# First MLP block in two halves of f around the second block, weight conversion without GpSimd, float32 on the first sequence's way back

## The chip, the cores and the metric

The kernel runs on one core of a Trainium2 chip. The metric is the device time of one execution in microseconds (us); lower is better. Five engines work side by side, each through its own list of instructions in the order in which the program writes them: TensorE (PE, matrix products), VectorE (DVE), ScalarE (ACT), GpSimd (POOL) and SyncE (SP, which here only starts DMA transfers). DMA transfers are also started by ACT and POOL. A transfer that waits for a buffer holds up whatever stands behind it on the engine that starts it.

## The reference, cut to what matters

```python
X = np.fft.rfft(x, axis=1)                       # x: 4 sequences of 3008 x 256, float32
Yr = Xr @ w_r - Xi @ w_i + b_r                   # 256 x 256 weights, complex product
Yi = Xr @ w_i + Xi @ w_r + b_i
Y = soft_shrink(Yr, 0.01) + 1j * soft_shrink(Yi, 0.01)
y = np.fft.irfft(Y, n=3008, axis=1)              # back to 12032 tokens of 256
h = y @ w_in                                     # 256 -> 2048
out = (h * sigmoid(h)) @ w_out                   # 2048 -> 256
```

w_in and w_out arrive as float64 and are brought to float32 pairs on the chip.

## The kernel before, in words

Each sequence goes through the spectral part and then, as rows of tokens, through the MLP. The transform of length 3008 is done as 47 x 64 in two matrix stages on each side:

- **s1** (lines 166 to 189; s1_half for sequences 2 and 3): eight groups g per sequence, two halves of 512 columns each; result to the scratch scr1 in device memory.
- **s2** and **mix** (lines 236 to 273): twelve steps u per sequence; s2 reads 256 KB of scr1 (tile a) and a 128 KB table (t2), splits its result into a high and a low float32r part (xh, xl), and mix multiplies by the complex weights in 24 products of 256 columns. VectorE then adds the bias and shrinks (lines 270 to 272, y).
- **i1**, the first stage of the way back (lines 353 to 374): split_z cuts y into zh (ScalarE) and zl (GpSimd for the first sequence, line 358), six float32r products with a split table t3 (256 KB, started by POOL), result to the scratch scr2.
- **i2** (lines 414 to 446): reads scr2 by groups of four j (tile gin, 384 KB) and writes the tokens of one MLP block, 512 columns, as xt (high and low).

The **MLP** runs in 24 blocks of 512 tokens (the last is smaller) with 16 slices f of 128 hidden units each. One pair (block, f) is a *tick*. In tick t the program emits, in this order: split_g of tick t-1 (gh on ScalarE, gl on VectorE, lines 477 to 485), mlp1 of tick t (six products of 512 columns, sigmoid on ScalarE, g on VectorE, lines 459 to 475), the *fill* of the tick, and mlp2 of tick t-2 (four pairs of products into four accumulators `acc`, lines 489 to 523). After f = 15 the four accumulators are copied and added (lines 519, 520) and stored.

Only the first sequence's spectral part (b = 0) and s1 of the second stand ahead of the ticks, in a *prologue*: s1 of sequence 0, then a loop of twelve u_steps, then a tail with the last i1 steps, s1(1,2) to s1(1,7) and the i2 of block 0. All other spectral work is fill: `put` gives each piece the next tick that has none (the list `taken`), `at` names a tick outright.

**Weight conversion** (lines 536 to 571): w_in and w_out come in 16 units of 512 KB, loaded by SP into buffers of tag gin (four) or s1o (two). w_begin loads the next unit and begins the oldest loaded one (ScalarE, line 558); the first w_go does two VectorE operations (lines 560, 561), the second w_go two more (lines 566, 567), a copy to the high part on ScalarE (line 569) and two GpSimd operations for the low part (lines 570, 571). Units 0 to 7 (f = 0 to 7) are converted in the prologue, units 8 to 15 in ticks 0 to 12, by the list W_PLAN of (w_go, w_begin) counts. A block needs all 16 f, so tick 8 of block 0 already needs unit 8.

x of sequences 0 and 1 is loaded by POOL (x_ahead, line 154) into seven buffers, chosen by X_BUFS; two of these are x_sb[0], x_sb[1].

Of the kernel before, what the change touches and what calls it, by code (L numbers as in the profile page):

```python
# [26 lines left out]
BLK = 512  # L27
NFF = DFF // 128
W_PLAN = [(1, 1), (1, 1), (1, 0), (2, 1), (1, 1), (1, 0), (1, 1), (3, 1), (0, 0), (1, 0), (1, 1), (2, 0), (1, 0)]
# [3 lines left out]
X_BUFS = [0, 1, 2, 3, 4, 5, 6, 0, 1, 2, 3, 4, 5, 2, 1, 0]  # L33
# [3 lines left out]
def dft_tables():  # L37
# [16 lines left out]
    for h in range(2):  # L54
# [33 lines left out]
    c3l = c3 - c3h  # L88
    return {
# [3 lines left out]
        "c4": c4.reshape(96, NP).astype(np.float32),  # L93
    }
# [3 lines left out]
def spectral_mlp_kernel(ctx: ExitStack, tc: tile.TileContext, x, w_r, w_i, b_r, b_i, w_in, w_out, c1, c2, c3, c4, out):  # L98
# [67 lines left out]
    def s1(b, g, late=False):  # L166
        t = x_t.pop((b, g))
        if b == 1 and g > 4:
            o = x_pre[(4, 6, 2)[g - 5]][:96, :]
        else:  # L170
            tag, bufs = ("s1o", 2) if 8 * b + g in (6, 7, 10, 11, 12) else ("gin", 4)
            o = sb.tile([128, 4 * D], F32, tag=tag, bufs=bufs, name="s1o")[:96, :]
# [180 lines left out]
    def split_z(b, u):  # L353
# [4 lines left out]
        (nc.gpsimd if b == 0 and u < NU - 2 else nc.vector).tensor_sub(zl, y, zh)  # L358
        u_t[b, u] = (zh, zl)

    def i1(b, u):
        zh, zl = u_t.pop((b, u))
# [3 lines left out]
        for r in range(2):  # L366
            for n, (m, z) in enumerate(((0, zh), (0, zl), (1, zh))):
                nc.tensor.matmul(  # L368
                    out=pv[:, r, :], lhsT=t3[:, m, r * 128:(r + 1) * 128], rhs=z[:, r, :],
                    start=(n == 0), stop=(n == 2),  # L370
                )
# [42 lines left out]
    def i2(i, e):  # L414

        c0, n = BLOCKS[i]
        if e == 0:
            xt[i] = tuple(sb.tile([128, 2, BLK], F32R, tag=f"xt{k}", bufs=2, name=f"xt{k}") for k in range(2))
# [70 lines left out]
    def mlp2(i, f):  # L489
        n = BLOCKS[i][1]  # L490
        gh, gl = gf.pop((i, f))
        for t in range(n // 128):
            if f == 0:
                acc[i, t] = ps.tile([128, 512], F32, tag="acc", bufs=4, name="acc")
            a = acc[i, t]
            q = slice(t * 128, (t + 1) * 128)
            if i == LAST:
# [8 lines left out]
                start=(f == 0), stop=False,  # L506
# [3 lines left out]
                start=False, stop=(f == NFF - 1),  # L510
            )
        if f == NFF - 1:
# [23 lines left out]
    def w64_load(src):  # L536
        tag, bufs = ("s1o", 2) if len(weights) < 6 and len(weights) % 3 else ("gin", 4)
        t = sb.tile([128, 512, 2], U32, tag=tag, bufs=bufs, name="w64")
# [8 lines left out]
    def w64_split(t, shape, hi, lo):  # L547
# [3 lines left out]
        def shaped(a):  # L551
# [10 lines left out]
                                       op0=ALU.bitwise_and, op1=ALU.bitwise_or)  # L562
        yield
# [5 lines left out]
        nc.scalar.copy(hi, w)  # L569
        nc.gpsimd.tensor_sub(w, w, hi)  # L570
        nc.gpsimd.tensor_tensor(out=lo, in0=w, in1=shaped(lw), op=ALU.add)

    with tc.manual_schedule():
# [6 lines left out]
        x_pre.extend(sb.tile([128, 4 * D], F32, tag=f"xt{k}", bufs=2, name="x_pre") for k in (0, 0, 1, 1))  # L580
# [65 lines left out]
        def u_step(b, u):  # L646
            if u < NU:
                if u + (3 if b == 0 else 2) < NU:
                    u_load(b, u + (3 if b == 0 else 2))
                s2(b, u)  # L650
            if u > 0:
                t3_load(b, u - 1)
            if b == 0:
                if u > 2:
                    w_go()
                if u % 2:
                    w_begin()
# [22 lines left out]
        for u in range(NU):  # L680
            u_step(0, u)
# [3 lines left out]
            if 1 < u < 8:  # L685
# [27 lines left out]
        i2(0, 1)
        w_begin()
        state["prologue"] = False

        ticks = [(i, f) for i in range(len(BLOCKS)) for f in range(NFF)]
# [5 lines left out]
        taken = set(range(17, len(ticks), NFF))  # L723
# [9 lines left out]
        for i in range(1, len(BLOCKS)):  # L733
            at(16 * i - 9, i2_load, i)
            put(16 * i - 7, i2, i, 0)
            put(16 * i - 5, i2, i, 1)
# [69 lines left out]
```

## Time and profile before

| what | value |
|---|---|
| median of 3 runs | 1387.65 us (1385.81 to 1388.34) |
| the profiled execution's own time | 1388.13 us |
| its span in the trace | 1386.3 us |
| mean granted TensorE clock | 0.994 |
| PE busy | 1364.3 us, 98% |
| DVE / ACT / POOL busy | 65% / 51% / 12% |
| chain of waits, by engine | PE 89%, DVE 4%, DMA 3%, issue 2%, ACT 1% |

The span runs from the first to the last instruction; the 1.83 us between it and the execution's own time lie around it. A PE that is busy is not PE at its peak: products overlap, so their shown durations are longer than the distance from one start to the next, and the distance is what counts. A granted clock of 1.00 is 2.4 GHz, and 0.5 is 1.2 GHz.

### The profile page before, as it was taken

The numbers are of one execution on the slowest core, as the hardware profiler recorded it, in microseconds if no ns is written. First come the engines' busy times: TensorE is split into PE (matmuls) and PEld (weight loads), VectorE is DVE, ScalarE is ACT, GpSimd is POOL, SyncE is SP. The second block draws the span as 40 slices with busy tenths as digits, with TensorE's granted clock in tenths as the row PEclk, the third lists the DMA queues.
The fourth block names the chain that finished last, engine by engine and source line by source line (L and its number), as shares of the span: only waits on it lengthen the run. The fifth ranks groups of instructions, "written<-read, shape, count | busy, mean of one in ns | idle before, by whom it ended". The sixth has DMA issues, their size and how long they took to land.

```text
span 1386.3 us, 20474 instructions
## 1 busy us (share of the span) xinstructions
PE 1364.3 (98%) x7638; PEld 1169.3 (84%) x7638; DVE 898.2 (65%) x1485; ACT 711.2 (51%) x1394; POOL 170.0 (12%) x205
## 2 busy tenths in 40 slices
PE   7998999999999999999999999999999999999998
PEld 3976788888888888888888888888888888888888
DVE  3899868777655677767655577776654555455555
ACT  5565555555554555555454445455444444444444
POOL 2555411120100011111100011111000000000000
PEclk9999999999999999999999999999999999999999
DMA  8975232331423214233121121220210110011001
GB/s 250 318 230 172 76 100 83 96 92 42 124 76 85 58 35 114 69 114 80 46 77 41 33 76 51 84 81 24 61 27 16 27 39 9 19 27 39 1 16 24
DMA packets 69855, 105.09 MB, mean 76 GB/s; under 512 B 7228, under 2 KB 51388, under 8 KB 69756
## 3 DMA queue, kind: packets, MB, share of 16 engines
q1 hardware_dynamic: 55685, 75.18, 18.5%
q0 software_dynamic: 10496, 24.91, 7.1%
q10 hardware_dynamic: 3575, 3.70, 0.8%
q8 instruction: 60, 0.98, 0.3%
q14 instruction: 39, 0.32, 0.1%
HBM read 66.28 MB, written 37.49 MB: 75 GB/s over the span
## 4 chain that ended last, share of the span: by engine, by line
PE 89%; DVE 4%; DMA 3%; issue 2%; ACT 1%; POOL 0%; ACTq 0%; SPq 0%; DVEq 0%; POOLq 0%
PE h L466 36%; PE acc L504 24%; PE acc L508 12%; PE mix L324 6%; PE i L410 3%; PE s L299 2%; PE i L368 2%; PE s L164 2%; PE acc L499 1%; DVE ww L560 1%; PE mix L263 1%; DMA scr<-i1o 1%; PE i2e L410 1%; DMA x_pre<-in_x_dram 1%; DVE gl L484 1%
## 5 line engine op out<-in xcount | busy, mean ns | idle before, releaser
L466 PE MATMUL h<-xt,win 128*128 128x512 f32 (+1 forms) x2304 | 588.5, 391 | 1.8 <-ACT xt L443 1.6
L504 PE MATMUL acc<-wout,gh 128*128 128x512 f32 x1472 | 540.0, 401 | 0.0
L466 PEld LDWEIGHTS h<-xt,win 128*128 128x128 f32 x2304 | 403.4, 189 | 85.3 <-ACT xt L443 1.7
L473 ACT ACTIVATE g<-h 128x512 f32<-128x512 f32 (+1 forms) x385 | 226.5, 588 | 387.6 <-PE h L466 386.3
L474 DVE TENSOR_TENSOR g<-h,g 128x512 f32<-128x512 f32 (+1 forms) x385 | 261.4, 679 | 242.2 <-ACT g L473 238.9
L508 PE MATMUL acc<-wout,gl 128*128 128x256 f32 x1472 | 413.0, 281 | 4.8 <-DVE gl L484 4.8
L484 DVE TENSOR_TENSOR gl<-g,gh 128x512 fp32r<-128x512 f32 (+1 forms) x385 | 282.1, 733 | 174.8 <-ACT gh L483 170.4
L504 PEld LDWEIGHTS acc<-wout,gh 128*128 128x128 f32 x1472 | 277.4, 188 | 59.0
L483 ACT CAST gh<-g 128x512 fp32r<-128x512 f32 (+1 forms) x385 | 235.1, 611 | 156.0 <-DVE g L474 153.6
L508 PEld LDWEIGHTS acc<-wout,gl 128*128 128x128 f32 x1472 | 278.6, 189 | 16.1 <-DVE gl L484 7.2
L331 POOL TENSOR_TENSOR q<-q,bias 128x256 f32<-128x256 f32 x36 | 26.4, 733 | 672.7 <-ACT q L330 672.7
L344 DVE TENSOR_TENSOR y<-q,mix 64x256 f32<-64x256 f32 x144 | 60.3, 419 | 2.2
L410 PEld LDWEIGHTS i<-c_sb,gin 96*128 96x128 f32 x420 | 54.4, 191 | 6.6 <-issue 1.7
L410 PE MATMUL i<-c_sb,gin 96*128 96x94 f32 x420 | 53.9, 272 | 1.6 <-DMA gin<-scr 1.6
L368 PE MATMUL i<-zh,t 128*128 128x256 f32 x192 | 45.4, 298 | 0.0
L299 PEld LDWEIGHTS s<-t,a 128*128 128x128 f32 x288 | 37.7, 191 | 3.0
L299 PE MATMUL s<-t,a 128*128 128x128 f32 x288 | 37.9, 274 | 0.0
L164 PE MATMUL s<-sx,c 94*96 94x512 f32 (+1 forms) x120 | 35.5, 404 | 1.0 <-DVE sx L195 0.3
L368 PEld LDWEIGHTS i<-zh,t 128*128 128x128 f32 x192 | 33.1, 190 | 1.1 <-issue 0.5
L520 DVE TENSOR_TENSOR o<-acc,o 128x256 f32<-128x256 f32 x92 | 32.4, 415 | 0.0
L332 POOL TENSOR_TENSOR q<-q,bias 128x256 f32<-128x256 f32 x36 | 32.0, 888 | 2.8
L426 DVE TENSOR_TENSOR xt<-i,xt 128x376 fp32r<-128x376 f32 (+2 forms) x48 | 28.0, 584 | 6.1 <-ACT xt L425 6.0
(113 smaller groups left out, 1232.3 us busy)
## 6 DMA issues: line engine op xcount, KB each, us to landing
a<-scr SPq DMA_DIRECT2D x48, 256.0 KB
t<-in_c_dram POOLq DMA_DIRECT2D x48, 256.0 KB, 3.2
gin<-scr SPq DMA_DIRECT2D x32, 384.0 KB
scr<-s1o SPq DMA_DIRECT2D x28, 384.0 KB
x_sb<-in_x_dram POOLq DMA_DIRECT2D x25, 376.0 KB, 4.4
scr<-i1o SPq DMA_DIRECT2D x36, 256.0 KB
t<-in_c_dram SPq DMA_DIRECT2D x48, 128.0 KB
w<-in_moe_w_in_dram SPq DMA_DIRECT2D x8, 512.0 KB
```

The source lines that it names most:

```text
L164: nc.tensor.matmul(out=p[:96, :], lhsT=c1_hl[m][:K, :], rhs=hl[k][:K, :], start=(n == 0), stop=(n == 2))
L299: nc.tensor.matmul(out=pv[:, e, :, r, :], lhsT=a[:, r, e * 128:(e + 1) * 128], rhs=t2[:, r * 128:(r + 1) * 128], start=True, stop=True,)
L324: nc.tensor.matmul(out=out, lhsT=x_[:, e, c, :], rhs=m[:, e, :], start=(n == 0), stop=(n == 5))
L368: nc.tensor.matmul(out=pv[:, r, :], lhsT=t3[:, m, r * 128:(r + 1) * 128], rhs=z[:, r, :], start=(n == 0), stop=(n == 2),)
L410: nc.tensor.matmul(out=p[:, o:o + m], lhsT=g_t[b, j // 4][:, q:q + 128], rhs=c4_sb[:, p0:p0 + m], start=True, stop=True,)
L466: nc.tensor.matmul(out=p[:, :n], lhsT=w[:, e, f * 128:(f + 1) * 128], rhs=v[:, e, :n], start=(m == 0), stop=(m == 5),)
L473: nc.scalar.activation(out=g[:, q], in_=p[:, q], func=ACTF.Sigmoid)
L474: nc.vector.tensor_tensor(out=g[:, q], in0=p[:, q], in1=g[:, q], op=ALU.mult)
L483: nc.scalar.copy(gh[:, q], g[:, q])
L484: nc.vector.tensor_sub(gl[:, q], g[:, q], gh[:, q])
L504: nc.tensor.matmul(out=a, lhsT=gh[:, q], rhs=wout[:, f].rearrange("p a c -> p (a c)"), start=(f == 0), stop=False,)
L508: nc.tensor.matmul(out=a[:, D:2 * D], lhsT=gl[:, q], rhs=wout[:, f, 0, :], start=False, stop=(f == NFF - 1),)
```

## The change: what it does

- The order of ticks becomes block 0 with f = 0 to 7, block 1 with all 16 f, block 0 with f = 8 to 15, then blocks 2 and up as before. The sums of the first half (f = 0 to 7) are added and kept in x_sb[1] and added to those of the second half at tick 33. i2 of block 1 moves from ticks 9, 11, 13 to ticks 1, 3, 5.
- The conversion's two last operations go from GpSimd to VectorE, and its high copy moves one w_go earlier. The units 8 to 15 are spread over ticks 0 to 19 (W_GO, W_BEGIN; the later entries find nothing left). Every unit is loaded into a gin buffer.
- For sequence 0, i1 is one float32 product per half instead of three float32r products, with an unsplit table (128 KB, started by SP); split_z is left out for it. i1(u-2) now stands in step u, where i1(u-3) stood.
- s1(1,5), s1(1,6), s1(1,7) move from the prologue's tail into six ticks (0, 2, 4, 6, 7, 8) as s1_later.
- The x loads of (1,2) to (1,6) stand in steps 3 to 7 of the loop; with no other work on POOL between them. s1 of sequence 2 starts at tick 37 instead of 30, with a spacing of 6 instead of 7.

```diff
+W_GO = (0, 1, 3, 4, 6, 7, 8, 9, 10, 12, 13, 14, 15, 17, 18, 19, 20, 21, 22)
+W_BEGIN = (1, 4, 7, 9, 12, 14, 17, 19)
-X_BUFS = [0, 1, 2, 3, 4, 5, 6, 0, 1, 2, 3, 4, 5, 2, 1, 0]
+X_BUFS = [0, 1, 2, 3, 4, 5, 6, 0, 1, 2, 3, 4, 0, 2, 1, 0]
...
+    def s1_later(g, i):
+        t = x_t[1, g]
+        if i == 0:
+            x_t[1, g, "o"] = sb.tile([128, 4 * D], F32, tag="s1o", bufs=2, name="s1o")[:96, :]
+        o = x_t[1, g, "o"]
+        p = bank("s1")
+        q = slice(i * 512, (i + 1) * 512)
+        nc.tensor.matmul(out=p[:96, :], lhsT=c1_sb, rhs=t[:, q], start=True, stop=True)
+        nc.scalar.copy(o[:, q], p[:96, :])
+        if i:
+            v = scr1[1].rearrange("r (a j) d -> (r a) (j d)", a=4)
+            store(v[:, g * 4 * D:(g + 1) * 4 * D], o)
+            del x_t[1, g], x_t[1, g, "o"]
...
     def t3_load(b, u):
+        if b == 0:
+            t3_t[b, u] = sb.tile([128, 256], F32, tag="t3", bufs=5, name="t3f")
+            nc.sync.dma_start(out=t3_t[b, u], in_=c3f[:, u * 256:(u + 1) * 256])
+            return
...
     def i1(b, u):
...
         for r in range(2):
+            q = slice(r * 128, (r + 1) * 128)
+            if b == 0:
+                nc.tensor.matmul(out=pv[:, r, :], lhsT=t3[:, q], rhs=z[:, r, :], start=True, stop=True)
+                continue
...
     def mlp2(i, f):
+        begins = f == 0 or (i, f) == (0, 8)
+        ends = f == NFF - 1 or (i, f) == (0, 7)
...
+        if ends:
             for t in range(n // 128):
                 a = acc.pop((i, t))
+                half = x_sb[1][:, t * D:(t + 1) * D]
+                if f == 7:
+                    nc.scalar.copy(half, a[:, D:2 * D])
+                    nc.vector.tensor_tensor(out=half, in0=a[:, 0:D], in1=half, op=ALU.add)
+                    continue
...
+                if i == 0:
+                    nc.vector.tensor_add(o, o, half)
...
     def w64_split(t, shape, hi, lo):
...
+        nc.scalar.copy(hi, shaped(w.bitcast(F32)))
         yield
...
-        nc.scalar.copy(hi, w)
-        nc.gpsimd.tensor_sub(w, w, hi)
-        nc.gpsimd.tensor_tensor(out=lo, in0=w, in1=shaped(lw), op=ALU.add)
+        nc.vector.tensor_sub(w, w, hi)
+        nc.vector.tensor_tensor(out=lo, in0=w, in1=shaped(lw), op=ALU.add)
...
+        def u_step(u):
             if u < NU:
+                if u + 3 < NU:
+                    u_load(0, u + 3)
+                t3_load(0, u)
+                s2(0, u)
+            if u > 1:
+                w_go()
+            if 0 <= u - 1 < NU:
+                mix(0, u - 1)
+            if u % 2 and u < NU:
+                w_begin()
             if 0 <= u - 2 < NU:
+                i1(0, u - 2)
...
+        w_begin()
+        u_step(NU)
         s1(1, 2)
+        flush(1)
+        u_step(NU + 1)
+        i2_load(0)
+        w_tags[:] = [(("zl", 2), ("zh", 2))]
+        s1(1, 3)
         w_go()
+        flush(1)
+        s1(1, 4)
         w_go()
         w_begin()
         i2(0, 0)
         i2_ends(0)
+        w_go()
         i2(0, 1)
+        i2_load(1)
+        w_go()
         w_begin()
+        flush(1)
...
+        ticks = [(0, f) for f in range(8)] + [(1, f) for f in range(NFF)] + [(0, f) for f in range(8, NFF)]
+        ticks += [(i, f) for i in range(2, len(BLOCKS)) for f in range(NFF)]
...
+        taken = {9, 25} | set(range(33, len(ticks), NFF))
...
+        for t in W_GO:
+            at(t, w_go)
+        for t in W_BEGIN:
+            at(t, w_begin)
+        for g in (5, 6, 7):
+            for i in range(2):
+                t = put(0, s1_later, g, i)
+            if g == 5:
+                at(t, x_ahead)
+        for t in (11, 35):
             at(t, x_ahead)
...
-        for b, t0, dt in ((2, 30, 7), (3, 110, 8)):
+        for b, t0, dt in ((2, 37, 6), (3, 110, 8)):
```

## Rows read from the trace of the kernel before

**Rows 1.** Busy time by stretch: PE, PEld, DVE, ACT, POOL (count), clock, DMA share, GB/s

```profile
40.40:88.80 48.40, 47.45 (x394) 46.51 (x393) 45.68 (x61) 28.59 (x60) 33.29 (x34) 1.00 1.03 295
...
107.67:165.00 57.33, 52.00 (x233) 41.29 (x234) 52.09 (x70) 28.86 (x54) 32.70 (x23) 0.91 0.43 133
165.00:1386.30 1221.30, 1216.80 (x6849) 1054.94 (x6847) 768.92 (x1312) 621.48 (x1222) 86.74 (x123) 1.00 0.21 57
```

**Rows 2.** PE's instructions by group, 107.67 to 165 us: count, busy, mean ns, idle

```profile
L466 PE MATMUL h<-xt,win 128*128 128x512 f32 x101 | 30.2, 441 | 1.8 <-ACT xt L443 1.6 <-ACT xt L425 0.2
L504 PE MATMUL acc<-wout,gh 128*128 128x512 f32 x56 | 21.7, 414 | 0.0
L508 PE MATMUL acc<-wout,gl 128*128 128x256 f32 x56 | 16.7, 298 | 4.8 <-DVE gl L484 4.8
```

**Rows 3.** Chain of waits in order of time, two neighbouring ticks: start, us, what

```profile
179.01 1.39 PE h L466 x6
181.79 1.39 PE h L466 x6
```

**Rows 4.** Busy time by stretch again, 126 to 130 us

```profile
126.00:130.00 4.00, 4.00 (x14) 3.26 (x13) 3.97 (x6) 1.76 (x5) 3.33 (x2) 0.57 0.41 123
```

**Rows 5.** DVE's instructions in order of time: start, us, what

```profile
113.27 0.69 DVE L484 TENSOR_TENSOR gl<-g,gh 128x512 fp32r<-128x512 f32 x1 [0.23 <-ACT gh L483]
...
123.23 1.63 DVE L561 SCALAR_TENSOR_TENSOR ww<-w,ww 128x512 uint32<-128x512 uint32 x1
...
127.04 1.77 DVE L484 TENSOR_TENSOR gl<-g,gh 128x512 fp32r<-128x512 f32 x1
```

**Rows 6.** POOL's instructions in order of time

```profile
122.99 1.33 POOL L571 TENSOR_TENSOR win<-ww,we 128x512 fp32r<-128x512 f32 x1
126.54 1.72 POOL L570 TENSOR_TENSOR ww<-ww,wout 128x512 f32<-128x512 f32 x1 [2.23 <-DVE we L566]
```

**Rows 7.** PE's instructions in order of time, loop and tail of the prologue

```profile
72.09 0.48 PE L263 MATMUL mix<-wr,xh 128*128 128x256 f32 x2
...
77.03 0.49 PE L263 MATMUL mix<-wr,xh 128*128 128x256 f32 x2
...
81.52 0.48 PE L263 MATMUL mix<-wr,xh 128*128 128x256 f32 x2
...
88.78 0.28 PE L368 MATMUL i<-zh,t 128*128 128x256 f32 x1
...
89.50 1.88 PE L183 MATMUL s<-x_pre,c_sb 128*96 128x512 f32 x4
...
96.27 5.31 PE L183 MATMUL s<-x_sb,c_sb 128*96 128x512 f32 x12
...
104.06 0.46 PE L410 MATMUL i<-c_sb,gin 96*128 96x94 f32 x2 [0.53 <-DMA gin<-scr]
...
107.67 0.50 PE L466 MATMUL h<-xt,win 128*128 128x512 f32 x1 [1.58 <-ACT xt L443]
```

**Rows 8.** ACT's instructions in order of time, around the same tail

```profile
40.55 0.68 ACT L558 ACTIVATE ww<-w 128x512 f32<-128x512 f32 x1 [2.34 <-DMA w<-in_moe_w_in_dram]
...
96.11 0.37 ACTq L135 DMA_DIRECT2D scr<-i1o  x1
...
106.42 0.62 ACT L569 CAST wout<-ww 128x512 fp32r<-128x512 f32 x1 [2.69 <-DVE ww L561]
```

**Rows 9.** POOL in order of time after the first weights' split

```profile
43.76 1.28 POOL L358 TENSOR_TENSOR zl<-y,zh 128x512 fp32r<-128x512 f32 x1 [10.64 <-ACT zh L357]
```

**Rows 10.** DMA, 32 to 44 us: packets, MB, mean rate

```profile
DMA packets 2586, 4.03 MB, mean 335 GB/s; under 512 B 247, under 2 KB 1889, under 8 KB 2585
```

**Rows 11.** DMA queues, 44 to 56 us: packets, MB, share of 16 engines

```profile
q0 software_dynamic: 504, 1.28, 44.3%
q1 hardware_dynamic: 1378, 1.59, 43.6%
```

**Rows 12.** DVE's instructions by group, 0 to 170 us: an accumulator's addition

```profile
L520 DVE TENSOR_TENSOR o<-acc,o 128x256 f32<-128x256 f32 x1 | 0.4, 415 | 0.0
```

More of the change, by code (lines that the diff above doesn't have):

```diff
@@ L88, in dft_tables @@
     c3l = c3 - c3h
+    c3f = c3
     return {
@@ L93, in dft_tables, with spectral_mlp_kernel @@
         "c4": c4.reshape(96, NP).astype(np.float32),
+        "c3f": c3f,
     }
 @with_exitstack
-def spectral_mlp_kernel(ctx: ExitStack, tc: tile.TileContext, x, w_r, w_i, b_r, b_i, w_in, w_out, c1, c2, c3, c4, out):
+def spectral_mlp_kernel(ctx: ExitStack, tc: tile.TileContext, x, w_r, w_i, b_r, b_i, w_in, w_out, c1, c2, c3, c4, c3f, out):
     nc = tc.nc
@@ L167, in s1 @@
         t = x_t.pop((b, g))
[L168 to L172, printed above, removed]
+        tag, bufs = ("s1o", 2) if 8 * b + g in (6, 7, 10, 11, 12) else ("gin", 4)
+        o = sb.tile([128, 4 * D], F32, tag=tag, bufs=bufs, name="s1o")[:96, :]
         for i in range(2):
@@ L357, in split_z @@
         nc.scalar.copy(zh, y)
-        (nc.gpsimd if b == 0 and u < NU - 2 else nc.vector).tensor_sub(zl, y, zh)
+        nc.vector.tensor_sub(zl, y, zh)
         u_t[b, u] = (zh, zl)
     def i1(b, u):
-        zh, zl = u_t.pop((b, u))
+        z = u_t.pop((b, u))
         t3 = t3_t.pop((b, u))
@@ L366, in i1 @@
         for r in range(2):
-            for n, (m, z) in enumerate(((0, zh), (0, zl), (1, zh))):
+            q = slice(r * 128, (r + 1) * 128)
+            if b == 0:
+                nc.tensor.matmul(out=pv[:, r, :], lhsT=t3[:, q], rhs=z[:, r, :], start=True, stop=True)
+                continue
+            for n, (m, k) in enumerate(((0, 0), (0, 1), (1, 0))):
                 nc.tensor.matmul(
-                    out=pv[:, r, :], lhsT=t3[:, m, r * 128:(r + 1) * 128], rhs=z[:, r, :],
-                    start=(n == 0), stop=(n == 2),
+                    out=pv[:, r, :], lhsT=t3[:, m, q], rhs=z[k][:, r, :], start=(n == 0), stop=(n == 2),
                 )
@@ L417, in i2 @@
         if e == 0:
-            xt[i] = tuple(sb.tile([128, 2, BLK], F32R, tag=f"xt{k}", bufs=2, name=f"xt{k}") for k in range(2))
+            v = "ab"[i > 0] if i < 3 else "ab"[(i + 1) % 2]
+            xt[i] = tuple(sb.tile([128, 2, BLK], F32R, tag=f"xt{v}{k}", bufs=1, name=f"xt{k}") for k in range(2))
         whole = [v for v in pieces(c0, n) if v[4] == NP]
@@ L536, in w64_load @@
     def w64_load(src):
-        tag, bufs = ("s1o", 2) if len(weights) < 6 and len(weights) % 3 else ("gin", 4)
-        t = sb.tile([128, 512, 2], U32, tag=tag, bufs=bufs, name="w64")
+        t = sb.tile([128, 512, 2], U32, tag="gin", bufs=4, name="w64")
         out = t.rearrange("p n two -> p (n two)")
@@ L579, in spectral_mlp_kernel @@
         x_pre.extend(x_sb)
-        x_pre.extend(sb.tile([128, 4 * D], F32, tag=f"xt{k}", bufs=2, name="x_pre") for k in (0, 0, 1, 1))
+        x_pre.extend(sb.tile([128, 4 * D], F32, tag=f"xt{k}", bufs=1, name="x_pre") for k in ("a0", "a1", "b0", "b1"))
         nc.sync.dma_start(out=c1_sb, in_=c1)
@@ L721, in at @@
             fill.setdefault(t, []).append((fn, args))
-        taken = set(range(17, len(ticks), NFF))
+        taken = {9, 25} | set(range(33, len(ticks), NFF))
         def put(t, fn, *args):
@@ L733, in spectral_mlp_kernel @@
         for i in range(1, len(BLOCKS)):
-            at(16 * i - 9, i2_load, i)
-            put(16 * i - 7, i2, i, 0)
-            put(16 * i - 5, i2, i, 1)
-            put(16 * i - 3, i2_ends, i)
-        for t, (go, begin) in enumerate(W_PLAN):
-            for _ in range(go):
-                at(t, w_go)
-            for _ in range(begin):
-                at(t, w_begin)
-        for t in (10, 11):
+            t = 16 * i - 9 if i > 1 else -1
+            if i > 1:
+                at(t, i2_load, i)
+            put(t + 2, i2, i, 0)
+            put(t + 4, i2, i, 1)
+            put(t + 6, i2_ends, i)
+        for t in W_GO:
[8 more added lines that the diff above has]
+        for t in (11, 35):
             at(t, x_ahead)
```

47 lines of the change are left out of this document (5 added, 42 removed).

## The prediction

> **What bounds the kernel now.** I read the busy time by stretch first. After 165 us PE is busy for 1216.80 of 1221.30 us at clock 1.00 [rows 1]: whatever happens to the other engines there, only PE's own work counts. From 107.67 to 165 us, which are the first ticks, PE is busy for 52.00 of 57.33 us at a mean clock of 0.91 while DVE is busy for 52.09 [rows 1]. That stretch holds 233 products: 101 of mlp1, 56 and 56 of mlp2 [rows 2] and 20 short ones of i2. A tick of six mlp1 and eight mlp2 products takes 2.78 us from one h group to the next, 1.39 for each half [rows 3]. So the work is 101/6 x 1.39 + 14 x 1.39 + 20 x about 0.11 = 23.4 + 19.5 + 2.2 = 45.1 us, and 57.3 - 45.1 = **12.2 us are lost**. Two things show in them. The waits for gl on DVE are 4.8 us [rows 2]. The clock falls to its lower level three times, each time a little after PE had stood still; one of the three is the stretch of 126 to 130 us with 0.57, that is 4 x 0.43 = 1.7 us lost [rows 4], so 5.2 in all. The rest are short waits.
>
> Why DVE is late: gl takes 0.69 us alone and 1.77 us beside a GpSimd operation on two SBUF tiles, and the conversion's line 561 takes 1.63 us beside line 571 [rows 5, 6]. Ahead of the ticks, from 40.40 to 88.80 us, DVE is full as well (45.68 of 48.40) but PE is 47.45 busy [rows 1], so the loop is PE's.
>
> **The change part by part.** The sum is made against the profiled execution: span 1386.3, own time 1388.13, which is 0.48 above the median. Gains are positive.
>
> *Loop of the first sequence.* i1 takes 0.72 us now (88.78 to 89.50) [rows 7]. In float32, twelve instructions of 512 columns take 5.31 us less the drain of the last, about 0.43 each [rows 7]; a float32 product is two instructions, so two products of 256 columns are 4 x 0.215 = 0.86 us. Up to the end of the last mix there will be ten i1 instead of nine: 8.6 - 6.5 = 2.1 us more. Against this, steps alternate between 4.94 (72.09 to 77.03) and 4.49 us (77.03 to 81.52) [rows 7], and the longer one waits for zl, which goes: 0.22 a step over some ten steps, 2.2. DVE takes two more operations per unit, 0.6 each at its issue distance, but none is stretched any more and y no longer waits behind a GpSimd operation; a pair of steps needs about 8 of 9.3 us on it. Sum 0; from -1 (waits stay in part) to +1.
>
> *The x loads.* POOL now stands for 10.64 us before its first zl at 43.76 [rows 9], so the x loads stand behind it. With zl and the t3 loads gone, nothing holds the five loads (5 x 376 KB = 1.88 MB, against 0.52 MB of t3 that leave) from going out together at about 32 us. DMA moves 4.03 MB in 32 to 44 us, 335 GB/s [rows 10]; 1.36 MB more are 4.1 us. ScalarE waits for unit 0 of the weights until 40.55 [rows 8], and the next step's xh stands behind it. Half of the engines' time for each queue, as in 44.3% and 43.6% where both had work [rows 11], puts unit 0 two to four us later; the i1 that now stands one step earlier gives PE 0.9 us and the old schedule 1.0 us of slack. I take -1.0, from 0 (all loads fit) to -4 (the full 4.1).
>
> The Trainium skill, "DMA: Bandwidth & Descriptors", section "Queues, rings and completion order", says that each DMA engine goes round between the queues that have work, a packet at a time. Rows 11 agree. By it alone unit 0 would wait the full half share, and the term would be near -2.
>
> *Tail of the prologue.* From the end of the last mix (88.78) to the first product of mlp1 (107.67) are 18.9 us [rows 7]. Its chain is y, zh and zl, i1, the store at 96.11 [rows 8], scr2 and back, 7.95 us later the last i2 columns at 104.06, and then ScalarE at 106.42 behind 2.69 us of DVE's conversion [rows 7, 8]. After: y is done 2.1 us after mix, i1 stands behind i1(10) and s1(1,2) and ends at 3.45, the store goes at 4.35 (7.3 now), scr2 and back 12.3, i2 of the whole block 14.2. The w_go between i2_ends and i2(0,1) puts a high copy on ScalarE that waits for two DVE operations, in front of the block's second copy: 16.2. Gain 18.9 - 16.2 = +2.7; from 0 (the DMA way back is as late as now) to +5 (the high copy is not in the way).
>
> *s1(1,5) to s1(1,7).* Twelve instructions, the 5.31 us group at 96.27 [rows 7], stood in the shadow of that way back. In the ticks PE has no such shadow: -5.2. Nothing covers it, so this bound is narrow (0.2).
>
> *The ticks.* Of VectorE alone, tick by tick from the new lists: g and gl are 1.2 us; the first w_go of a unit about 1.1; the second, now four operations, 2.3; i2 about 0.5 each. Ticks 0 to 9 sum to 29 us against PE's 10 x 2.78 + 5.2 + 2.0 = 35; ticks 10 to 19 to 25 against 28. So PE leads in both, where now 13 ticks hold eight conversions. What stays lost: one low-clock stretch after the idle gap that the missing s1 leaves in the tail, 1.7 to 3.4, take 2.5; tick 9, where the four operations (2.3) stand in front of the four additions of 0.415 [rows 12] that free the accumulators for tick 10: 1.4; the load of i2(1)'s third group behind a weight unit, 0.5; others 0.5. Together 4.9, gain 12.2 - 4.9 = **+7.3**, from 0 (the loss stays 12.2) to +10 (2 stay).
>
> *SP's queue.* It takes the twelve t3 loads (half the bytes they had on POOL) and, with every unit in a gin buffer, stands at a unit's load until an older unit's last read on DVE. Behind it stand the next a and t2 loads, which are asked for three steps ahead, t3, wanted two steps later, and in the ticks the stores of s1(1), wanted at tick 18. I cost it at 0; where that lead is gone, the next step is as late as the unit's conversion, some 1 us, in the margins above.
>
> *Everything else.* Four copies and eight small additions for the halves lie under PE. From tick 40 on the pieces stand in the same ticks as before but for one place in the row of s1(2). 0, at most 0.5 either way.
>
> Sum: 0 - 1.0 + 2.7 - 5.2 + 7.3 + 0 = **+3.8 us**. Span 1382.5, own time 1384.3, and from the median 1387.65 - 3.8 = 1383.8.
>
> **The rivals.**
>
> *All of it is gained.* The x loads do no harm, the high copy is not in the way (+5), 2.5 us stay lost in the ticks: 0 + 5 - 5.2 + 9.7 = +9.5, 1378. For it: DVE has slack on average in every group of ticks. Against it: tick 9 and the idle gap in the tail are in the program's order.
>
> *The x loads take the gain.* The stall reaches 3 us and the clock falls once more after it, as it did after the waits in the ticks [rows 4]: -4.7 in place of -1.0, 1387.5, no change. For it: the 335 GB/s of [rows 10] are close to all that DMA gives in this prologue. Against it: slack of 1.9 us.
>
> *VectorE stays the bound in the first ticks (slower).* Two more operations per unit on the engine that was already full, 16 x 0.6 = 9.6 us in the ticks. If gl comes after mlp2's turn in most conversion ticks, stalls bring the low clock as now, the loss stays 12.2 and the s1 products come on top: -1.0 + 2.7 - 5.2 = -3.5, 1391.2. It decides from a loss of 8.7 us in the ticks, where the whole sum is 0. For it: 3.5 us of DVE in a 2.8 us tick at 12, 14, 17 and 19. Against it: a whole tick of slack between split_g and its mlp2, and none of the operations is stretched.
>
> **How the numbers follow.** Chances: the forecast 0.50, all gained 0.20, x loads 0.15, VectorE 0.15. Faster or slower by over 0.2% (2.8 us, about what a measurement of this kernel tells from no change) means below 1384.9 or above 1390.4. The forecast's own range is 1381 to 1387, so some two thirds of it are faster and a third is the same: 0.34 and 0.16. With the rivals: faster 0.34 + 0.20 + 0.02 = 0.56, same 0.16 + 0.12 + 0.02 = 0.30, slower 0.14. The range runs from 1378.5, inside the all-gained case, to 1390.0, short of the VectorE case.
>
> **What would show it.** Right: first mlp1 product near 106 us or earlier, no GpSimd arithmetic between 35 us and tick 18, gl at 0.69 us throughout, PE's waits for gl under 1 us in the first 20 ticks, one clock drop in place of three, twelve float32 s1 instructions between h groups. Wrong: a wait of PE for xl at 43 to 48 us over 2 us (x loads); the first product at 107 us or later (tail); DVE waits of several us with clock drops between ticks 8 and 20 (VectorE); or a slower row after 165 us, for which I see no cause.

## The result and the profile after

| | before | after |
|---|---|---|
| median of 4 runs each, us | 1387.94 | **1398.18** (1395.70 to 1399.53) |
| the profiled execution's own time, us | 1388.13 | 1399.53 |
| its span, us | 1386.3 | 1397.8 |
| PE / DVE / ACT / POOL busy | 98 / 65 / 51 / 12% | 98 / 64 / 50 / 7% |

The ratio is 1.0079, 95% interval 1.0067 to 1.0092: slower by 0.8%, where 1383.8 us was forecast and 1390.0 was the upper end. Busy shares, as so often, tell nothing of it. Busy time by stretch does (PE, PEld, DVE, ACT, POOL, clock, DMA share, GB/s). After's stretches that answer to [rows 1] are the loop from the first s2 to the end of the last mix, the tail up to the first mlp1 product, the first ticks and the rest:

```profile
31.07:94.48 63.41, 58.74 (x424) 56.94 (x425) 43.84 (x76) 27.80 (x58) 2.79 (x6) 0.92 0.81 245
94.48:114.12 19.64, 12.74 (x47) 8.46 (x45) 10.23 (x19) 7.39 (x15) 0.52 (x1) 0.80 0.55 173
114.12:175.00 60.88, 55.06 (x253) 43.26 (x253) 47.50 (x82) 30.30 (x61) 3.77 (x4) 0.95 0.44 134
175.00:1397.80 1222.80, 1217.10 (x6843) 1054.96 (x6841) 775.57 (x1326) 621.95 (x1225) 86.42 (x124) 1.00 0.21 56
```

The same view of after in its two longest stretches at the lower clock level (1.2 GHz), one in the loop and one in the tail:

```profile
44.80:51.60 6.80, 5.16 (x20) 4.83 (x21) 2.52 (x5) 2.63 (x6) 0.00 (x0) 0.50 1.02 382
106.20:116.40 10.20, 7.71 (x30) 7.01 (x31) 3.15 (x7) 2.67 (x6) 0.00 (x0) 0.50 0.49 174
```

Three places make the 11.5 us of span. The last mix ends at 94.48 instead of 88.78 [rows 7]: +5.7. From there to the first mlp1 product it is 19.6 us instead of 18.9: +0.7. From that product to the end it is 1283.6 instead of 1278.7: +5.0, just what the twelve s1 products cost, so the ticks gained nothing. The last stretch, after 175 us, is PE's as before.

**The loop.** After's POOL in order of time (start, us, what): its x loads go out together, where it stood waiting for zl before [rows 9], and the last line shows how long it then has nothing else to do.

```profile
31.29 1.04 POOL L153 DMA_DIRECT2D x_pre<-in_x_dram  x2
32.33 1.53 POOL L153 DMA_DIRECT2D x_sb<-in_x_dram  x3
...
102.12 0.52 POOL L153 DMA_DIRECT2D x_sb<-in_x_dram  x1 [68.27 <-PE s L184]
...
168.82 2.73 POOL L307 TENSOR_TENSOR w32d<-w 128x512 f32<-128x512 f32 x2 [23.95 <-DMA bias<-in_b_i_dram]
```

After's DMA queues in 35 to 42 us (packets, MB, share of 16 engines); q0 holds the x loads:

```profile
q0 software_dynamic: 411, 1.40, 86.1%
q1 hardware_dynamic: 328, 0.30, 19.1%
```

After's PE in order of time, the first i1 of the loop and i2 in the tail:

```profile
46.44 2.04 PE L389 MATMUL i<-y,t3f 128*128 128x256 f32 x4 [4.58 <-DMA t3f<-in_c3f_dram]
...
108.29 1.99 PE L433 MATMUL i<-c_sb,gin 96*128 96x94 f32 x8 [6.46 <-issue]
110.68 0.74 PE L433 MATMUL i<-c_sb,gin 96*128 96x94 f32 x2 [0.41 <-DMA gin<-scr]
```

After's ACT in order of time (answer to [rows 8]): unit 0, the last store of the tail, and two copies in the ticks:

```profile
47.57 0.66 ACT L590 ACTIVATE ww<-w 128x512 f32<-128x512 f32 x1 [10.45 <-DMA w<-in_moe_w_in_dram]
99.13 0.38 ACTq L139 DMA_DIRECT2D scr<-i1o  x1
...
147.55 0.62 ACT L595 CAST wout<-ww 128x512 fp32r<-128x512 f32 x1 [3.47 <-DVE ww L593]
148.56 0.62 ACT L507 CAST gh<-g 128x512 fp32r<-128x512 f32 x1
```

All five x loads are under way by 34 us. Their queue takes 86% of the DMA engines. The first t3 (SyncE starts it at 34.44) lands only at 46.4 and PE stands 4.58 us for it; unit 0 of the weights comes 7.0 us later than before (47.57 against 40.55, [rows 8]). From 44.8 us, still within that stall, the clock is at its lower level for 6.8 us.

**The ticks.** After's PE groups in 114.12 to 175 us (answer to [rows 2]: count, busy, mean ns, idle):

```profile
L490 PE MATMUL h<-xt,win 128*128 128x512 f32 x102 | 28.8, 421 | 0.0
L530 PE MATMUL acc<-wout,gh 128*128 128x512 f32 x59 | 24.6, 447 | 3.7 <-DVE x_sb L544 3.7
L534 PE MATMUL acc<-wout,gl 128*128 128x256 f32 x58 | 17.0, 292 | 2.2 <-DVE gl L508 2.1
L200 PE MATMUL s<-x_sb,c_sb 128*96 128x512 f32 x12 | 6.1, 592 | 0.0
```

After's waits of ScalarE in the same stretch (us, times, longest):

```profile
ACT win L595 <- DVE ww L593: 11.2, 4, 4.2
ACT wout L595 <- DVE ww L593: 6.2, 3, 3.5
ACT gh L507 <- DVE g L498: 3.7, 4, 2.5
```

The reader is to see that PE's waits hardly shrank (5.9 us here, 4.8 for gl before) although VectorE is less busy (47.5 of 60.9 us; 52.1 of 57.3 before) and gl is no longer stretched. After's DVE in order of time (answer to [rows 5]):

```profile
149.21 0.69 DVE L508 TENSOR_TENSOR gl<-g,gh 128x512 fp32r<-128x512 f32 x1 [1.69 <-ACT gh L507]
...
152.81 1.41 DVE L544 TENSOR_TENSOR x_sb<-acc,x_sb 128x256 f32<-128x256 f32 x4
...
169.14 1.26 DVE L599 TENSOR_SCALAR we<-ww 128x512 uint32<-128x512 uint32 x1
170.44 1.66 DVE L600 SCALAR_TENSOR_TENSOR we<-w,we 128x512 f32<-128x512 uint32 x1
```

gl takes 0.69, but it waits for ScalarE, and ScalarE waits 17.4 us for line 593: the high copy is now issued right behind the two VectorE operations that make its input, ScalarE takes its list in order, and gh and the next sigmoid stand behind it.

### The profile page after: what moved, and what is told of

It reads as the page before. It is cut to its first block, busy times and chain, and to the rows that moved or that the text cites. A ratio compares the mean times of both kernels' runs of the same rounds, so it can differ in the third digit from the quotient of the medians.

```text
span 1397.8 us, 20349 instructions
## 1 busy us (share of the span) xinstructions
PE 1367.3 (98%) x7614; PEld 1173.4 (84%) x7614; DVE 890.1 (64%) x1523; ACT 704.5 (50%) x1386; POOL 100.6 (7%) x151
## 4 chain that ended last, share of the span: by engine, by line
PE 90%; DVE 4%; DMA 3%; ACT 1%; issue 1%; SPq 0%; ACTq 0%; DVEq 0%
PE h L490 36%; PE acc L530 24%; PE acc L534 12%; PE mix L344 6%; PE i L433 3%; PE s L319 2%; PE i L392 2%; PE s L168 2%; DMA t3f<-in_c3f_dram 1%; PE acc L525 1%; PE i2e L433 1%; DMA x_pre<-in_x_dram 1%; DMA gin<-scr 1%; PE mix L283 0%; DMA t<-in_c_dram 0%
## 5 line engine op out<-in xcount | busy, mean ns | idle before, releaser
L508 DVE TENSOR_TENSOR gl<-g,gh 128x512 fp32r<-128x512 f32 (+1 forms) x385 | 276.6, 719 | 182.8 <-ACT gh L507 177.8
L392 PE MATMUL i<-zh,t 128*128 128x256 f32 x144 | 33.7, 297 | 1.4 <-issue 1.4
L449 ACT CAST xt<-i 128x376 fp32r<-128x376 f32 (+2 forms) x48 | 24.2, 503 | 20.9 <-PE i L433 20.9
```

The costliest lines, as they stand in the source:

```text
L392: nc.tensor.matmul(out=pv[:, r, :], lhsT=t3[:, m, q], rhs=z[k][:, r, :], start=(n == 0), stop=(n == 2),)
L508: nc.vector.tensor_sub(gl[:, q], g[:, q], gh[:, q])
```

## The experiments

Ratios are to the kernel before, with their 95% interval. Unless said otherwise a kernel is the changed one with the edit shown. Three causes of the loss were in question: the x loads let go at once, the early high copy, and the way back through scr2 in the tail. Each expectation names its own theories.

### The x loads (e4, e1, e6)

e4 puts the burst alone into the kernel before:

```diff
+        for _ in range(6):
+            x_ahead()
         for u in range(NU):
...
-            if 1 < u < 8:
-                x_ahead()
```

> The kernel before with one edit: its six x loads of the loop stand in front of the loop on POOL, behind the split of w_i, so that they go out together at about 32 us. Theory A (such a burst by itself holds up the loop): the last mix ends 3 to 6 us later than 88.8 and the time is 1391 to 1394. Theory B (only the t3 loads on SP make it late): within 1 us of the kernel before, 1387 to 1389.

Measured: 1394.00 us, 1.0053 (1.0038 to 1.0068), +6.6 us. The last mix stands 5.5 us later (93.82 against 88.3), and from the first mlp1 product on the time is the same (1278.6). The burst costs its price with nothing else changed.

e1 paces the loads by putting the loop's five on SyncE's queue:

```diff
-                x_ahead()
+                x_ahead(nc.sync)
```

> The changed kernel with one edit: the five x loads inside the first loop are started by SP, in the order of the program behind each step's a and t2 loads, instead of by POOL. Theory A (the loads go out together at 31 us because nothing on POOL holds them, and take DMA from t3 and from weight unit 0): PE's wait of 4.6 us for t3f and the clock's fall at 44.8 us go, ScalarE waits under 3 us for unit 0 (10.45 now), the last mix of the loop ends near 89 us (94.5 now), time 1398.2 - 6 = about 1392. Theory B (t3 is late because it stands on SP's queue behind other loads, whoever loads x): the wait stays at 3 us or more, time 1397 to 1398.

Measured: 1425.22, 1.0279 (1.0263 to 1.0294). A miss as an edit: the loads of 94 rows stood in front of t3 and a. e1's waits of PE:

```profile
PE i L389 <- DMA t3f<-in_c3f_dram: 16.4, 4, 5.4
```

e1's SyncE in order of time, one transfer behind such a load:

```profile
53.32 7.61 SPq L246 DMA_DIRECT2D t<-in_c_dram  x1
```

The stall at 42 us was gone, the first wait for t3f came at 65 us, with the loads. It shows where the loads must not go, not what the burst costs.

e6 leaves them on POOL and gives POOL something to wait for, one element per partition of y of the step before:

```diff
+    def gate(v):
+        nc.gpsimd.tensor_tensor(out=gate_t, in0=v, in1=v, op=ALU.add)
...
             if 2 < u < 8:
+                gate(u_t[0, u - 1][:, 0, 0:1])
                 x_ahead()
```

> The changed kernel with one edit: ahead of each of the loop's five x loads POOL does a 128x1 addition that reads the y of the step before, so that one load goes out per step instead of five at 31 us; they stay on POOL's queue (from SP they stood in the way of the step's own loads). Theory A (the burst is the loss of the loop): no wait for t3f over 0.5 us, unit 0 waited for under 3 us, the last mix ends at 88 to 89.5, time 1398.2 - 6 = 1392. Theory B (t3 on SP's queue is what is late): the wait for t3f stays over 3 us, time within 1 us of 1398.

Measured: 1395.16, 1.0060 (1.0045 to 1.0075). PE's wait for t3f is gone and the last mix starts 6.1 us earlier (87.86 against 94.00), the first mlp1 product 6.2 us earlier. Yet the profiled execution is only 4.1 us shorter and the median 3.0: from the first mlp1 product to the end it takes 2.1 us longer (1285.8). Those 2.1 us don't lie where the conversion runs. After's busy time from the first mlp1 product to the sigmoid of tick 40, and from there to the end:

```profile
114.12:266.00 151.88, 144.69 (x770) 121.74 (x770) 120.26 (x211) 78.85 (x162) 17.77 (x23) 0.97 0.35 101
266.00:1397.80 1131.80, 1127.48 (x6326) 976.47 (x6325) 702.82 (x1196) 573.40 (x1125) 72.42 (x105) 1.00 0.20 54
```

The same two stretches of e6:

```profile
107.91:259.70 151.79, 144.88 (x770) 121.53 (x770) 120.05 (x211) 78.82 (x162) 17.84 (x23) 0.97 0.36 101
259.70:1393.70 1134.00, 1129.68 (x6326) 975.95 (x6325) 702.48 (x1196) 572.94 (x1125) 72.50 (x105) 1.00 0.20 54
```

The first stretch is equal in both. The second is 2.2 us longer in e6, with the same work at clock 1.00, and the difference is spread over all of it: two neighbouring mlp1 products start 229.2 ns apart in the mean instead of 227.3. Every kernel here that has the gate's 128x1 constant shows it (1133.9 to 1134.0 us behind tick 40), also h3 below, which never calls the gate; before, after and e1 to e5 show 1131.3 to 1131.9. So these 2.2 us go with the constant, not with the loads; why a constant does this isn't shown. The burst's harm is shown, and nothing of what its removal gains is given back in the first 40 ticks.

### The high copy (e5, f1)

```diff
         nc.vector.scalar_tensor_tensor(out=w, in0=high, ...)
-        nc.scalar.copy(hi, shaped(w.bitcast(F32)))
         yield
+        nc.scalar.copy(hi, shaped(w.bitcast(F32)))
```

> The changed kernel with one edit: the conversion's high copy on ScalarE stands at the start of the second w_go again, not at the end of the first. Theory A (in the first w_go the copy waits on ScalarE for the two VectorE operations issued just before it, 3.47 us at 147.6, and gh and the sigmoid stand behind it, so gl and with it mlp2 are late): the waits at 153 us (3.65) and 174 us (2.06) shrink to under 2 and 0.5, time 1398.2 - 3 to - 5, about 1394. Rival (VectorE's own queue is late whatever ScalarE does): within 0.8 us of the changed kernel.

Measured: 1390.53, 1.0024 (1.0014 to 1.0033), 7.7 us less than the change; first mlp1 product to end 1276.1, that is 7.5 less. e5's waits of ScalarE in 112 to 173 us:

```profile
ACT gh L507 <- DVE g L498: 13.2, 8, 3.9
ACT g L497 <- PE h L490: 9.9, 12, 1.7
```

e5's waits of PE in the same stretch:

```profile
PE acc L530 <- DVE x_sb L544: 1.4, 1, 1.4
PE acc L534 <- DVE gl L508: 1.0, 1, 1.0
```

The waits for line 593 are gone, PE's fall from 5.9 to 2.4 us. The high copy is the largest single term.

f1 puts e6 and e5 together.

> The changed kernel with two edits: paced x loads in the loop and the high copy at the start of the second w_go. Theory A (two losses apart from each other; the paced loads alone gave 2.4 because what the loop saved, 6.1 us, went to waits behind the high copy in the ticks): both count in full, 1397.6 - 7.1 - 6 = about 1384.5. Rival (the first ticks end when the conversion ends, whenever they begin): no better than the high copy alone, 1390 to 1391.

Measured: 1388.38, 1.0008 (0.9999 to 1.0018): the two gains, 3.0 and 7.7, nearly add up (9.8), and bring it back to the kernel before. The 1384.5 of theory A is not reached: beside the high copy the paced loads give 2.2 us, with the 2.2 us of the gate's constant already taken off. Its profiled execution (1392.8) is the slowest of its eleven and has a low clock for 13.7 us from 102.1 us, in the tail and the first ticks.

### Order in the ticks (e2, e3)

e2 takes the second w_go of a unit off tick 9, where it stood ahead of the additions; e3 moves two of m3's steps (the GpSimd operations at 168.82 above):

```diff
-W_GO = (0, 1, 3, 4, 6, 7, 8, 9, 10, 12, ...
+W_GO = (0, 1, 3, 4, 6, 7, 8, 10, 11, 12, ...
```
```diff
-        for t in (15, 18, 21):
+        for t in (15, 22, 25):
```

> The changed kernel with one edit: the second w_go of unit 11 stands in tick 10 and the first of unit 12 in tick 11, so no conversion stands in tick 9, in front of the four additions that free the accumulators. Theory A (that order costs PE the 3.65 us at 153 us and the clock's fall at 154 us behind it): wait under 0.5 us there, one clock fall less, time about 1398.2 - 4.5 = 1393.7. Rival (VectorE is behind through all of these ticks): the wait turns up again one or two ticks later, time 1397 to 1398.5.

> The changed kernel with one edit: the two later steps of the mix weights for the other sequences, with their GpSimd operations, stand in ticks 22 and 25 instead of 18 and 21, behind the last conversion. Theory A (the two GpSimd operations at 168.8 us stretch the conversion's 0.42 and 0.69 us operations to 1.26 and 1.66 and so cause PE's 2.06 us wait at 174 us and the clock's fall at 174.5): the wait and the fall go, time about 1398.2 - 3.5 = 1394.7. Rival (the wait comes from ScalarE's high copy that stands in front of gh): no change within 0.7 us.

Measured: e2 1396.15, 1.0063 (1.0046 to 1.0080); e3 1398.30, 1.0083 (1.0068 to 1.0098). In e2 the wait for the additions falls from 3.7 to 1.3 us but waits for gl grow to 3.5: some 2 us at most. e3 changes nothing.

### The tail (e7, e8)

e7 issues the stores of s1(1,3) and s1(1,4) on SyncE behind scr2's loads instead of on ScalarE's queue, and gates the load of x(1,7) until a tick:

```diff
-        s1(1, 3)
+        s1(1, 3, late=True)
...
-        s1(1, 4)
+        s1(1, 4, late=True)
...
+                at(t, lambda: gate(gf[0, 2][:, 0:1]))
                 at(t, x_ahead)
```

> The changed kernel with one edit in the tail's DMA: the stores of s1(1,3) and s1(1,4) go out on SP behind the scr2 loads instead of at once on ScalarE's queue, and x(1,7) is held until tick 2 by a 128x1 addition on POOL. Theory A (scr2's way back is 11.5 us instead of 7.95 because these 1.1 MB move beside it): first i2 product 105 to 106 in place of 108.3, time 1398.2 - 3 = 1395. Rival (the way back itself is slow, or the clock): first i2 product within 0.5 us of 108.3, no change in time.

Measured: 1396.35, 1.0067 (1.0052 to 1.0082). Tail and first ticks of e7, busy time by stretch:

```profile
92.62:109.32 16.70, 12.16 (x51) 8.12 (x49) 10.70 (x20) 7.34 (x15) 0.00 (x0) 0.90 0.50 160
109.32:170.00 60.68, 55.03 (x259) 43.07 (x259) 47.85 (x82) 30.45 (x62) 4.49 (x6) 0.97 0.48 148
```

From the start of the last mix to the first mlp1 product it is 16.7 us instead of 20.1, so the tail's loss is real. From there to the sigmoid of tick 40 it is 150.6 us instead of 151.9: nothing is given back there. Behind tick 40 stand the 2.2 us of the gate's constant. The medians differ by 1.8 us, and the two intervals overlap, so the gain at the end isn't clear of the noise. Which of the two edits helped isn't separated.

e8 is e6 and e7's late stores with the products of s1(1,5) to s1(1,7) back in the tail (their outputs in three of the x buffers), six paced loads instead of five, and s1_later out of the ticks; only the first is shown:

```diff
+        s1(1, 5, late=True)
+        flush(1)
+        s1(1, 6, late=True)
+        s1(1, 7, late=True)
```

> The changed kernel with the paced x loads (six in the loop), and with s1(1,5) to s1(1,7) back in the prologue's tail, their results in x buffers, stores of s1(1,3) to s1(1,7) on SP behind the scr2 loads. Theory A (those products were free in the tail, cost 5.2 us of PE in the ticks, and their absence lets the clock fall for 10.2 us): against the run with paced x loads alone 5.2 + 3 = 8 us less, about 1384, and no low clock from 106 to 116 us. Rival (the products, copies and stores hold up i2 by as much as they save): within 1.5 us of the run with paced loads alone, about 1391.

Measured: 1391.17, 1.0036 (1.0024 to 1.0048). The first mlp1 product comes at 102.8 us, earlier than in any kernel so far, and there is no low clock around it. But it takes 1286.1 us from there to the end, though 5.2 us of products left the ticks: 2.2 us more behind tick 40, as in every kernel with the gate's constant, and 152.2 up to it against 151.9 in the change. So it is 4.0 us less than e6, half of theory A's 8. e8's waits of PE:

```profile
PE acc L533 <- DVE x_sb L547: 4.0, 1, 4.0
PE acc L537 <- DVE gl L511: 3.7, 7, 1.7
```

The sigmoid of tick 10 in the change:

```profile
151.69 0.61 ACT L497 ACTIVATE g<-h 128x512 f32<-128x512 f32 x1
```

and in e8:

```profile
140.24 0.63 ACT L500 ACTIVATE g<-h 128x512 f32<-128x512 f32 x1
```

It comes 37.6 us after the first mlp1 product in the change (114.12) and 37.5 in e8 (102.76), with the products of s1 in these ticks and without them; e5, with the late copy, takes 35.3. With the early high copy, the conversion's chain over VectorE and ScalarE sets the pace there, not PE: what PE is spared waits in the ticks.

### All together, and parts undone (f2, f3, h1 to h4, g1)

f2 is e6, e7, e5 and e2; f3 is e8, e5 and e2.

> The same two edits and two more: the late stores of s1(1,3) and s1(1,4) with x(1,7) held, and no conversion in tick 9. Theory A: 3.4 us of the tail and 1.4 us at tick 10 less than with the two edits, about 1380. Rival (the tail's gain is given back in the ticks, as when it was tried alone): 1383 to 1385.

> The changed kernel with paced x loads, s1(1,5) to s1(1,7) back in the tail with late stores, the high copy in the second w_go and no conversion in tick 9. Theory A (in the ticks without those products VectorE has less cover: eight conversions and g, gl need 54 us in 20 ticks against PE's 57): about 1380, as good as with them in the ticks. Rival (the idle gap of the tail is pure loss and nothing else): 5 us better than with them in the ticks, 1375 to 1377.

Measured: f2 1383.32, 0.9975 (0.9964 to 0.9985). **f3 1377.73, 0.9933 (0.9920 to 0.9947)**, faster than both kernels. f2 has the time of its rival, but not its reason: from the first mlp1 product on it takes 1279.3 us, f1 1280.0, so nothing is given back; it is 5.1 us below f1, and f1 had missed its own 1384.5. f3 is 5.6 us below f2, as its rival had it. Busy time by stretch in f3 (from the start of the last mix to the first mlp1 product, first ticks, rest):

```profile
85.25:100.58 15.33, 15.33 (x62) 8.42 (x61) 9.68 (x19) 10.09 (x19) 0.00 (x0) 1.00 0.62 198
100.58:165.00 64.42, 62.48 (x317) 51.40 (x317) 61.35 (x108) 37.19 (x73) 4.57 (x4) 1.00 0.50 142
165.00:1374.20 1209.20, 1203.51 (x6767) 1041.01 (x6765) 762.42 (x1303) 613.35 (x1209) 86.70 (x124) 1.00 0.20 56
```

f3's DMA queues in 35 to 42 us:

```profile
q1 hardware_dynamic: 994, 2.09, 91.3%
```

PE is full in the tail and 62.5 of 64.4 us in the first ticks, at clock 1.00 in each of these stretches; the one low stretch left (3.4 us from 28.7) stands at the loop's start. SyncE's queue has the DMA engines to itself in the 7 us that the burst took.

Each of the next undoes one part in f3, so that a part's price is read with the rest repaired. h2 puts the high copy back where the change has it; h3 takes the gates of the loop away; h4 restores the old order of ticks (blocks one after the other, the old W_PLAN); h1 gives the two low operations back to GpSimd:

```diff
-        nc.vector.tensor_sub(w, w, hi)
-        nc.vector.tensor_tensor(out=lo, in0=w, in1=shaped(lw), op=ALU.add)
+        nc.gpsimd.tensor_sub(w, w, hi)
+        nc.gpsimd.tensor_tensor(out=lo, in0=w, in1=shaped(lw), op=ALU.add)
```

g1 does what h1 does, on f1.

> The repaired kernel with the high copy back at the end of the first w_go, as in the change. If the place of this copy is what kept the loss of the ticks at 12 us: 6 to 9 us slower, 1384 to 1387, with waits of PE for gl and the additions in the first 20 ticks. If its effect came from the bad start of the ticks alone: within 2 us of 1377.7.

> The repaired kernel with the six x loads of the loop let go at once. If the burst is a loss by itself: 5 to 7 us slower, 1383 to 1385, last mix 6 us later. If what it delays is made up later, as it seemed with the late copy alone: within 2 us.

> The repaired kernel with the order of ticks, the i2 places and the conversion plan of the kernel before (block 0 with all 16 f first, eight units in 13 ticks), still without GpSimd in the conversion. If the two halves are what frees VectorE in the first ticks: 6 to 10 us slower, 1384 to 1388, waits for gl between ticks 0 and 13. If GpSimd's absence does it: within 2 us of 1377.7.

> The repaired kernel (paced x loads, s1 in the tail, high copy in the second w_go, tick 9 free; 1377.7) with the conversion's two last operations back on GpSimd. Theory A (stretched VectorE operations cost more than the two extra ones): 3 us or more slower, 1381 or above. Theory B (VectorE has 20 ticks and is not the bound any more, so either place will do; where VectorE is nearly full, two operations less help it): 1376 to 1379. Theory C (the removal is itself a loss): 1375 or below.

> The run with paced x loads and late high copy, with the conversion's two last operations back on GpSimd. Theory A (a GpSimd operation on two SBUF tiles stretches VectorE's, so that taking it away is a gain though VectorE does two operations more): 3 to 6 us slower than without GpSimd, clock falls in the ticks as in the kernel before. Rival (the removal is worth nothing, the spread over 20 ticks does it all): within 1 us.

| kernel | median, us | ratio to before (95%) | against f3 |
|---|---|---|---|
| h2, high copy early | 1389.85 | 1.0019 (1.0010 to 1.0028) | +12.1 |
| h3, x burst | 1383.62 | 0.9978 (0.9969 to 0.9988) | +5.9 |
| h4, old order of ticks | 1388.92 | 1.0017 (1.0008 to 1.0025) | +11.2 |
| h1, low part on GpSimd | 1379.80 | 0.9948 (0.9935 to 0.9960) | +2.1 |
| g1, low part on GpSimd (in f1) | 1385.14 | 0.9982 (0.9973 to 0.9991) | f1 is 1388.38 |

h2's waits of ScalarE in its first ticks, the same signature as in the change:

```profile
ACT wout L598 <- DVE ww L596: 11.5, 4, 5.2
ACT win L598 <- DVE ww L596: 10.1, 4, 3.4
```

So the order in halves, with the conversion spread over 20 ticks that it allows, is worth 11 us once the copy and the loads no longer eat it; it was the part with the merit. h4 has the low part on VectorE as f3 has, and the repaired kernel in the old order with the low part on GpSimd wasn't run: the 11 us hold for a conversion without GpSimd. h2 and h4 cost more than expected (12.1 for 6 to 9, 11.2 for 6 to 10).

Moving the low part off GpSimd is worth nothing that these runs agree on: 2.1 us with overlapping intervals in f3, 3.2 us of the other sign in f1, which neither theory of g1 had. From the first mlp1 product to the end f3 and h1 take the same (1273.6 and 1273.7 us); what parts them lies ahead of it, where f3 and f4 below, with the same program up to there, are 3.2 us apart as well. f1 and g1 take 1280.0 and 1277.4: in those ticks PE waits 1.4 us for the additions of tick 9 and 1.0 for gl in f1, and for neither in g1. f1 still has the conversion in tick 9, f3 hasn't. That this turns the sign is likely, but wasn't tested.

### A miss (f4)

f4 repeats e3's edit in f3.

> The repaired kernel with the GpSimd operations for the mix weights in ticks 22 and 25 instead of 18 and 21. Its one wait of PE for gl over 0.5 us in the ticks (1.69 us at 149.8) stands behind two such operations at 145 us. Theory A (they stretch the conversion beside them, and alone in the changed kernel this was hidden behind the high copy): the wait goes, 1.5 to 2 us faster, ratio to the kernel before about 0.992. Rival (the wait has another cause): no change, 0.9933.

Measured: 1376.89, 0.9926 (0.9912 to 0.9940), the same as f3. The trace says why neither tested what it meant to. f4's GpSimd in order of time:

```profile
148.50 3.34 POOL L310 TENSOR_TENSOR w32d<-w 128x512 f32<-128x512 f32 x2 [34.74 <-DMA w<-in_w_i_dram]
```

f4's VectorE at the same moment:

```profile
148.91 1.78 DVE L605 TENSOR_TENSOR ww<-ww,win 128x512 f32<-128x512 f32 x1
```

A later tick doesn't hold GpSimd: it runs ahead of the others to the next thing it must wait for, here a transfer, and the operation ran where that landed, beside the conversion (1.78 us instead of 0.69). In e3 the two operations ran at 168.37, in the change at 168.82. A gate in front of it wasn't tried.

## Why the prediction was wrong, by its steps

**The x loads: -1.0 forecast, -4 as the bound.** The whole loop, i1 included, came out -5.7, or -6.4 if counted from its first s2. The mechanism was named, its size was not. The failed step is "half of the engines' time for each queue, as in 44.3% and 43.6%" [rows 11]: it was 86.1% to 19.1%. The queues did take turns, but nearer to packet for packet: 411 against 328, of 3.4 KB (1.40 MB / 411) and 0.9 KB (0.30 MB / 328). A queue with packets nearly four times as long takes the time. The equal shares of [rows 11] came with 504 against 1378 packets; they were no sharing rule. The Trainium skill, "DMA: Bandwidth & Descriptors", section "Queues, rings and completion order", states the turn by packets. The counts of 35 to 42 us roughly fit it; by it q0 can't have had work throughout in [rows 11], so "Rows 11 agree" doesn't hold, and equal time was my own reading of it. The place was wrong too: the prediction looked for the delay at unit 0 and for a wait of PE for xl. Unit 0 did come 7.0 us later, but PE stood for t3f, on SyncE's queue, which the prediction costed at 0. Then 1.9 us of slack couldn't cover 7 us of delay: 4.6 us of stall and 3.4 of the 6.8 at half clock, less the 1.7 that a shorter low stretch at the loop's start gives back (3.4 us there, 6.8 before), make 6.3 of the 6.4. This is the rival "the x loads take the gain", at a higher price than its -4.7.

**i1 in float32 at 0.** With the gate (e6) it is 57.4 us from the first s2 to the last mix (30.49 to 87.86), against 56.6 before (31.74 to 88.3): the 0 holds within its bound in this execution. In the ten kernels with gated loads the loop takes 55.8 to 59.7 us to the end of the last mix, 57.8 in the mean, against 57.2 before, so one execution doesn't tell 1 us. The edit wasn't run alone.

**The tail: +2.7 forecast, -0.7 measured.** The store went out 4.65 us after the last mix (4.35 forecast), and i2's last columns to the first mlp1 product took 3.4 us (3.9 forecast). The failed step is the way back, taken over at 7.95 us: it was 11.55 (99.13 to 110.68). Those 3.6 us are the whole miss. Beside it stood what the old tail didn't have there: the stores of s1(1,3) and s1(1,4), and x(1,7), which POOL issued at 102.12. PE, idle meanwhile, then ran i2 at the low clock. e7 takes 3.4 of it back.

**s1(1,5) to s1(1,7): -5.2.** The change's ticks are 5.0 us longer at an unchanged loss, which fits. The price wasn't read alone: f2 and f3, which differ in little else, are 5.7 us apart from the first mlp1 product on, but f2 spends its first 4.8 us there at half the clock, 2.4 us lost, and f3 none. f2 from the first mlp1 product:

```profile
102.59:107.38 4.79, 4.79 (x11) 3.02 (x11) 3.81 (x7) 2.37 (x5) 0.00 (x0) 0.50 0.45 113
```

It doesn't add to the rest where PE isn't the bound: from e6 to e8 the ticks lose these products and get no shorter.

**The ticks: +7.3 forecast, 0 measured.** The step that failed is the list by VectorE alone. It was right of VectorE: it has slack, gl is 0.69, and e5 shows a loss of 1276.1 - (1278.7 + 5.2 - 12.2) = 4.4 us where 4.9 were forecast. But the chain goes through ScalarE, in order, and the early high copy makes it wait there 17.4 us for VectorE. The prediction saw this wait once, in the tail, priced it, and didn't carry it to the eight units of the ticks. Tick 9, at 1.4 us, cost 3.7 for the same reason (1.4 in e5). The third rival's loss of 12 us came true, and its mark of DVE waits with clock drops, but not its cause as it was put: with the two operations left on VectorE the loss falls to 4.4 when the copy alone is moved (e5). That these operations cost nothing isn't shown: h1 and f3 are alike in the ticks, g1 is 2.6 us shorter there than f1.

**The sum.** The terms were added as if each kept its price. Where another engine sets the pace they don't: e8 takes 5.2 us off PE ahead of tick 10 and reaches that tick no sooner after its first mlp1 product. e8, e5 and e2 give 7.0, 7.7 and 2.0 us alone, 16.7 in sum, and 20.5 together in f3. That e6 ends with less than it saves ahead of the ticks has another reason, the 2.2 us of the gate's constant, which f3 still pays.

## What to carry to other kernels

When an operation is moved earlier, look at the engine that takes it in order: how long until its input is there, and what stands behind it, in every place where the list is used. When an engine loses its work, ask what had held its DMAs back; here only a data dependence held them, not their place in the program (e3, f4, and the x loads). When an edit gains less at the end than where it was made, compare stretch by stretch: here the rest lay in ticks that the edit doesn't touch. A part that measures as a loss inside a bundle may be its best part (here the halves), so undo parts in the repaired kernel before judging them.

## What was not expected of the hardware

Two queues shared the DMA engines nearer to equal packets than to equal time, in three kernels in 35 to 42 us: 411 to 328 packets with 86.1 to 19.1% of the time (after), 403 to 323 with 83.5 to 20.0% (h3), 404 to 439 with 74.3 to 28.0% (e4). A VectorE operation beside one on GpSimd takes 2.4 to 2.6 times as long (1.66 and 1.78 us against 0.69 both), yet moving eight units' low parts between the two engines changed the whole by 2 to 3 us at most, with either sign. And one more 128x1 constant put mlp1's products 229.2 ns apart instead of 227.3 behind tick 40, 2.2 us in all, in each of the twelve kernels that have it and in none of the other seven; the cause is open.
